# Fused block-sparse attention and squared-ReLU feed-forward: the weights in eight large loads ahead of the second batch, and the last outputs in two PSUM banks

## The chip, the cores and the metric

The kernel runs on one core of one Trainium2 chip. The metric is the device time of one execution in microseconds, the median of three runs. A profile is one further execution, recorded by the hardware profiler.

## The reference

Attention with a block mask comes first: a query block of 32 rows sees its neighbours, the first and last block, and three sampled blocks; the first and last block see all. Then a feed-forward network with a squared ReLU:

```python
# q, k, v: (4, 8, 768, 64) f32; w_in: (512, 2048); w_out: (2048, 512)
scores = scale * np.matmul(q, k.transpose(0, 1, 3, 2))
scores = np.where(mask, scores, -1000000000.0)
attn = softmax(scores)                       # written out in the reference
x = np.matmul(attn, v).transpose(0, 2, 1, 3).reshape(B * S, H * D)
h = x @ w_in
r = np.maximum(h, 0.0)
out = (r * r) @ w_out                        # (3072, 512) f32
```

## The kernel before, in words

**Attention.** A unit is one pair of heads of one batch; there are 16, numbered 0 to 15, four to a batch. Three loads of 384 KB bring a unit's q, k and v (SP's queue; `load`, L142 to L144). VectorE casts q and k to bf16 (L241), TensorE transposes them (L253), VectorE copies the transposes out of PSUM (L260) and casts v (L247; for units 1 to 3 GpSimd does that). The mask is added by 24 (or 64) more rows of the matmul's contraction; each buffer set AA, BB needs these rows once, and sets 1 to 5 get them by copies from set 0 (`static_rows`, L233 and L234). The scores of 256 queries against 256 keys, two heads (L288, L290), go through one exp on ScalarE (L295) into the product with v (L308, L310); a column of ones in VA and VB gives the softmax's sums, ScalarE forms their inverse (L317 to L319) and VectorE multiplies (L328, L329) into xT, the transposed input of the feed-forward. There are 144 such score steps, nine to a unit. In the first batch the four units alternate by query range; afterwards one unit follows another.

**Feed-forward.** xT is cut in nine token tiles T0 to T8: three of 256 tokens for batch 0, two of 384 for each later batch. For each of 16 column blocks f of w_in, `hidden` (L343) is four matmuls into one of two PSUM buffers of the pool `h`, which the transposes also use; VectorE takes max(h, 0) into one of four `r` buffers (L349); GpSimd squares it into `g` (L355). For each 128 tokens, `output` (L363) is 16 matmuls in four parts into the one PSUM buffer `y`; ScalarE copies it out (L368) and SP stores it (L372).

**Weights.** w_in and w_out are read as f32 and cast to bf16 by the DMA itself, which only GpSimd's queue issues. There are 8 loads for w_in (L273) and 8 for w_out (L276), 256 KB each as they land. A GpSimd load takes one of eight semaphores; the ninth load waits until the first has landed.

**What sets the order.** A planner in the kernel (`run_schedule`) holds one task for each of these steps with its engine, an estimated duration, what it depends on, buffers taken and given back, and a key. It always takes the task that can start first on its model clock, and among equals the lowest key; attention has lower keys than the feed-forward, so that the feed-forward fills gaps. The order is fixed when the program is built: on the chip, each engine takes its instructions strictly in that order, and waits at each for what it needs.

Of the kernel before, what the change touches and what calls it, by code (L numbers as in the profile page):

```python
# [12 lines left out]
F32 = mybir.dt.float32  # L13
BF = mybir.dt.bfloat16
# [5 lines left out]
P = 128  # L20
# [5 lines left out]
def kernel(  # L26
# [16 lines left out]
    nc = tc.nc  # L43
# [4 lines left out]
    d_model = H * D  # L48
# [4 lines left out]
    HP = H // 2  # L53
    NF = d_ff // P
# [11 lines left out]
    ps_o = ctx.enter_context(tc.psum_pool(name="ps_o", bufs=1))  # L66
    ps_h = ctx.enter_context(tc.psum_pool(name="ps_h", bufs=2))
    ps_y = ctx.enter_context(tc.psum_pool(name="ps_y", bufs=1))
    ctx.enter_context(tc.manual_schedule())


# [2 lines left out]
    tasks = []  # L74

    class Task:
        def __init__(self, eng, us, key, fn, deps=(), get=None, put=(), after=0.0, late=0.0):
            self.eng, self.us, self.key, self.fn = eng, us, key, fn
            self.deps, self.get, self.put = list(deps), get, list(put)
            self.after, self.late = after, late  # L80
            self.end = self.free = None
            self.order = len(tasks)
            self.holds = 0
            for t in self.put:
                t.holds += 1
            tasks.append(self)
# [14 lines left out]
                    r = max(r, old.free)  # L101
            return r

    def run_schedule(free, bufs):

        taken = {name: [] for name in bufs}
        left = {e: [t for t in tasks if t.eng == e] for e in free}
        while any(left.values()):
            best = None
            for e, ts in left.items():  # L110
                cand = [(max(r, free[e]), t) for t in ts
                        for r in (t.ready(taken, bufs),) if r is not None]
                if cand:
                    at = min(c[0] for c in cand)
                    t = min((c[1] for c in cand if c[0] <= at + 1e-9), key=lambda t: (t.key, t.order))
                    if best is None or at < best[0]:
                        best = (at, t)
            assert best is not None, "no task can start"
            at, t = best
            t.end = free[t.eng] = at + t.us  # L120
            if t.get:
                taken[t.get].append(t)
            for p in t.put:
                p.holds -= 1
                p.free = max(p.free or 0.0, t.end + t.late)
            left[t.eng].remove(t)
            t.fn()
        return max(free.values())
# [102 lines left out]
    def static_rows(i):  # L231

        nc.sync.dma_start(out=AA[i][64:64 + nb], in_=AA[0][64:64 + nb])  # L233
        nc.sync.dma_start(out=BB[i][0:64], in_=BB[0][0:64])  # L234
# [29 lines left out]
    w_out_sb = consts.tile([P, NF, d_model], BF, name="w_out_sb")  # L264
    wiv = moe_w_in.rearrange("(k p) f -> p k f", p=P)
    wov = moe_w_out.rearrange("(n p) d -> p n d", p=P)
    NWP = 8

    def w_load(i):

        if i < NWP:
            fs = slice(i * d_ff // NWP, (i + 1) * d_ff // NWP)
            nc.gpsimd.dma_start(out=w_in_sb[:, :, fs], in_=wiv[:, :, fs])  # L273
        else:
            n0 = (i - NWP) * 2
            nc.gpsimd.dma_start(out=w_out_sb[:, n0:n0 + 2, :], in_=wov[:, n0:n0 + 2, :])  # L276


    ptile, stile, otile, rtile, xT = {}, {}, {}, {}, {}
# [59 lines left out]
    def hidden(T, f):  # L339
        b, c0, w = T  # L340
        ph = ps_h.tile([P, TWM], F32, name="ph", tag="h")[:, 0:w]
        for kc in range(KM):
            nc.tensor.matmul(ph, w_in_sb[:, kc, f * P:(f + 1) * P], xT[b][:, kc, c0:c0 + w],  # L343
                             start=(kc == 0), stop=(kc == KM - 1))
        htile[T, f] = ph
# [6 lines left out]
    def square(T, f):  # L352
# [2 lines left out]
        G.tensor_mul(out=g, in0=r, in1=r)  # L355
        gtile[T, f] = g

    def output(T, ts, part):
        if part == 0:
            ytile[T, ts] = ps_y.tile([P, d_model], F32, name="py", tag="y")  # L360
        py = ytile[T, ts]
        for f in range(part * NF // NY, (part + 1) * NF // NY):
            nc.tensor.matmul(py, gtile[T, f][:, ts * P:(ts + 1) * P], w_out_sb[:, f, :],  # L363
                             start=(f == 0), stop=(f == NF - 1))
# [22 lines left out]
    pe = dict(late=0.2)  # L387
# [5 lines left out]
    ev, cv, sc_of, va_of, mu = {}, {}, {}, {}, {}  # L393
    for u in range(NU):
        sc_of[u], va_of[u] = [], []
    wl, tr = {}, {}

    def prepare(u):
        s0 = first[u]
        if u < HP:  # L400
            ld_t = None
        else:

            ld_t = Task("SP", 1.3, s0 - 20, (lambda u=u: load(u, nc.sync)),
                        deps=cv[u - HP] + tr[u - HP], late=6.5)
        c = {}
        tr[u] = []
        old = sc_of[u - NPB] if u >= NPB else []
        for w in (1, 0):
            kw = dict(deps=[ld_t] + old) if ld_t else dict(after=arrive[u][w])  # L410
            c[w] = Task("DVE", 0.57, s0 - 6, (lambda u=u, w=w: cast_qk(u, w)), get="qc", **kw, **SEM)
            tr[u].append(c[w])
        ev[u] = []
        for w in (1, 0):
            t = Task("PE", 0.34, s0 - 4 - w, (lambda u=u, w=w: transp(u, w)), deps=[c[w]],
                     get="h", put=[c[w]], **pe)
            for h in range(2):
                ev[u].append(Task("DVE", 0.57, s0 - 4, (lambda u=u, w=w, h=h: evac(u, w, h)),
                                  deps=[t], put=[t], **SEM))
        kw = dict(deps=[ld_t]) if ld_t else dict(after=arrive[u][2])  # L420
        kw.setdefault("deps", [])
        if u >= NPB:
            kw["deps"] += va_of[u - NPB]
        vfull = u in range(1, HP)
        cv[u] = [Task("POOL" if vfull else "DVE", 0.9 if vfull else 0.36, s0 - 2,
                      (lambda u=u, h=h: cast_v(u, h)), **kw, **SEM) for h in range(2)]
        if u == HP - 1:

            for i in range(2 * NWP):
                wl[i] = Task("POOL", 1.15, s0 + i, (lambda i=i: w_load(i)),  # L430
                             deps=cv[u], late=4.0 + 0.8 * i)
        if HP <= u < NPB:
            early = [Task("SP", 0.9, s0 - 8, (lambda u=u: static_rows(u)), after=36.0, late=5.0),
                     Task("POOL", 0.7, s0 - 8, (lambda u=u: init_v(G, u)), after=36.0, **SEM)]
        else:
            early = []
        return early
# [27 lines left out]
    for k, T in enumerate(TILES + [None]):  # L465
        hs = [(T, f) for f in range(NF)] if T else []
        ys = [(TILES[k - 1], ts, part) for ts in range(TILES[k - 1][2] // P) for part in range(NY)] if k else []
        both = [((i + 0.5) / len(hs), 0, x) for i, x in enumerate(hs)]
        both += [((i + 0.5) / len(ys), 1, x) for i, x in enumerate(ys)]
        for _, kind, x in sorted(both, key=lambda e: e[:2]):  # L470
            n_key += 1
            T_ = x[0]
            b, c0, w = T_
            if kind == 0:
                f = x[1]
                need = [mu[b * HP + a, qi] for a in range(HP)
                        for qi in range(c0 // QW, (c0 + w - 1) // QW + 1)]
                hh = Task("PE", SQ[w][0], n_key, (lambda x=x: hidden(*x)), deps=need + [wl[f // 2]],
                          get="h", **pe)
                rr = Task("DVE", SQ[w][1], 0, (lambda x=x: relu(*x)), deps=[hh], get="r", put=[hh], **SEM)  # L480
                sq_of[x] = Task("POOL", SQ[w][2], n_key, (lambda x=x: square(*x)), deps=[rr], get="g",
                                put=[rr], **SEM)
            else:
                _, ts, part = x
                fs = range(part * NF // NY, (part + 1) * NF // NY)
                last_ts = ts == w // P - 1
                yy = Task("PE", 0.862, n_key, (lambda x=x: output(*x)),
                          deps=[sq_of[T_, f] for f in fs] + [wl[NWP + f // 2] for f in fs] + ([yprev] if part else []),
                          get=None if part else "y", put=[sq_of[T_, f] for f in fs] if last_ts else [], **pe)
                yprev = yy  # L490
                if part == 0:
                    yhead = yy
                if part == NY - 1:
                    yc = Task("ACT", 0.59, 0, (lambda T_=T_, ts=ts: out_copy(T_, ts)), deps=[yy], get="ys",
                              put=[yhead], **SEM)
                    Task("SP", 0.5, 0, (lambda T_=T_, ts=ts: store(T_, ts)), deps=[yc], put=[yc], late=2.0)

    run_schedule({"PE": 6.0, "DVE": 5.1, "ACT": 7.8, "POOL": 9.0, "SP": 12.0},
                 {"ps": 2, "po": 1, "h": 2, "y": 1, "pT": PT_BUFS, "r": R_BUFS, "g": G_BUFS, "ys": 3,
                  "qc": 3})  # L500


# [28 lines left out]
```

## Time and profile before

| | |
|---|---|
| median of 3 runs | 351.83 us (351.08 to 352.35) |
| the profiled execution, its own time | 353.31 us |
| its span, first to last instruction | 351.6 us |
| TensorE (PE) busy | 318.0 us, 90% |
| ScalarE (ACT) busy | 209.9 us, 60% |
| VectorE (DVE) busy | 183.6 us, 52% |
| GpSimd (POOL) busy | 136.2 us, 39% |
| mean granted TensorE clock | 0.975 |
| DMA moved | 31.10 MB |

The profile's page gives busy shares over the whole span, a strip of 40 slices of 8.8 us, and the costliest groups of instructions with the idle time before them. The chain of waits is followed back from the last instruction to what released each. Busy time of PE counts a matmul to its modelled end: a 256-column matmul lasts 0.27 us there, though the next one can start 0.11 us later, so PE can lose time while it counts as busy. Matmuls of different kinds are therefore counted, and multiplied by their spacing, where PE's work is needed.

### The profile page before, as it was taken

Reading aid. Unit: us, or ns where it says so; the run is one execution under the profiler, and the core shown is the slowest. Engines: PE = TensorE matmul, PEld = TensorE weight load, DVE = VectorE, ACT = ScalarE, POOL = GpSimd, SP = SyncE. Lnnn points to the kernel's source line nnn. Section 1 sums busy time; section 2 is a strip of 40 time slices with the busy share of each in tenths; the row PEclk is TensorE's granted clock in tenths of the full one; section 3 lists DMA queues with packets and bytes.
Section 4 is the critical chain, followed back from the end, with each engine's and each line's share of the span. In section 5 each row is a group of like instructions: output and inputs, shape, how many; then the busy total and the mean of one; then the engine's idle time right before and its main releaser. Section 6 shows DMA issues by size and latency. Waiting matters only on the chain.

```text
span 351.6 us, 5958 instructions
## 1 busy us (share of the span) xinstructions
PE 318.0 (90%) x2306; PEld 219.3 (62%) x2306; DVE 183.6 (52%) x378; ACT 209.9 (60%) x315; POOL 136.2 (39%) x191
## 2 busy tenths in 40 slices
PE   2878850889999999999999999999999999999994
PEld 1656730666878777767777667676766755555541
DVE  7779301797867676449695433434343354444310
ACT  3688780178777686877768786787878732100011
POOL 8354125311635233105444323233233345666610
PEclk9999985699999999999999999999999999999999
DMA  7999999716622220010000000000000000010011
GB/s 249 274 323 300 285 270 206 165 59 211 208 93 79 88 76 0 34 52 8 1 2 0 32 30 2 30 32 0 33 30 3 30 32 30 30 62 30 32 60 60
DMA packets 23556, 31.10 MB, mean 88 GB/s; under 512 B 1584, under 2 KB 20016, under 8 KB 23528
## 3 DMA queue, kind: packets, MB, share of 16 engines
q1 hardware_dynamic: 16856, 26.13, 23.0%
q0 software_dynamic: 6400, 4.20, 8.0%
q8 instruction: 18, 0.29, 0.4%
q10 hardware_dynamic: 272, 0.39, 0.3%
q14 instruction: 10, 0.08, 0.1%
HBM read 27.26 MB, written 6.29 MB: 95 GB/s over the span
## 4 chain that ended last, share of the span: by engine, by line
PE 76%; DMA 11%; POOL 3%; ACT 3%; DVE 3%; SPq 2%; issue 1%; ACTq 0%; DVEq 0%
PE py L363 23%; PE ph L343 22%; DMA w_in_sb<-in_moe_w_in_dram 8%; PE po L308 8%; PE po L310 7%; PE ps L288 7%; PE ps L290 7%; DMA vs<-in_v_dram 2%; PE pt L253 2%; POOL w_in_sb L273 2%; ACT pT L295 1%; POOL g L355 1%; DVE r L349 1%; ACT ys L368 1%; SPq L233 0%
## 5 line engine op out<-in xcount | busy, mean ns | idle before, releaser
L295 ACT ACTIVATE pT<-ps 128x1024 bf16<-128x1024 f32 x144 | 141.8, 1017 | 65.1 <-PE po L310 57.1
L355 POOL TENSOR_TENSOR g<-r 128x384 bf16<-128x384 f32 (+1 forms) x144 | 111.0, 778 | 166.2 <-DVE r L349 166.1
L349 DVE TENSOR_SCALAR r<-ph 128x384 f32<-128x384 f32 (+1 forms) x144 | 73.1, 512 | 117.3 <-PE ph L343 79.6
L343 PE MATMUL ph<-xT,w_in_sb 128*128 128x384 bf16 (+1 forms) x576 | 104.0, 310 | 1.6 <-DMA w_in_sb<-in_moe_w_in_dram 1.0
L363 PE MATMUL py<-w_out_sb,g 128*128 128x512 bf16 x384 | 97.8, 381 | 1.7 <-ACT ys L368 1.4
L288 PE MATMUL ps<-AA 88*128 88x256 bf16 x288 | 73.8, 279 | 3.9 <-ACT pT L295 2.6
L343 PEld LDWEIGHTS <-w_in_sb 128*128 128x128 bf16 x576 | 56.2, 98 | 29.1 <-DMA w_in_sb<-in_moe_w_in_dram 1.2
L290 PE MATMUL ps<-BB 128*128 128x256 bf16 x288 | 73.5, 279 | 0.5 <-DVE BB L260 0.3
L308 PE MATMUL po<-pT,VA 128*128 128x256 bf16 x288 | 70.9, 274 | 3.2 <-ACT pT L295 2.3
L310 PE MATMUL po<-pT,VB 128*128 128x256 bf16 x288 | 70.9, 274 | 0.0
L363 PEld LDWEIGHTS <-g 128*128 128x128 bf16 x384 | 37.4, 98 | 34.2 <-issue 2.3
L368 ACT COPY ys<-py 128x512 f32<-128x512 f32 x24 | 14.1, 586 | 58.7 <-PE py L363 58.7
L308 PEld LDWEIGHTS <-VA 128*128 128x128 bf16 x288 | 28.2, 98 | 13.3 <-issue 4.3
L290 PEld LDWEIGHTS <-BB 128*128 128x128 bf16 x288 | 28.9, 100 | 10.4 <-issue 3.9
L288 PEld LDWEIGHTS <-AA 88*128 88x128 bf16 x288 | 28.8, 100 | 8.7 <-POOL VB L174 1.5
L310 PEld LDWEIGHTS <-VB 128*128 128x128 bf16 x288 | 28.2, 98 | 9.2 <-issue 1.6
L253 PE MATMUL pt<-identb,qc 128*128 128x128 bf16 x192 | 17.6, 236 | 13.4 <-DVE qc L241 13.3
L328 DVE TENSOR_TENSOR xT<-po,rs 64x256 bf16<-64x256 f32 x48 | 19.9, 414 | 16.9 <-ACT rs L319 16.1
L253 PEld LDWEIGHTS <-qc 128*128 128x128 bf16 x192 | 14.1, 106 | 17.6 <-DVE qc L241 16.1
L260 DVE COPY AA<-pt 64x768 bf16<-64x768 bf16 x32 | 17.6, 549 | 11.9 <-PE pt L253 11.3
L317 ACT ACTIVATE ls<-po 64x256 f32<-64x256 f32 x48 | 18.3, 381 | 7.7 <-PE po L310 6.6
L319 ACT ACTIVATE rs<-ls 128x256 f32<-128x256 f32 x48 | 20.0, 416 | 1.5
(46 smaller groups left out, 126.3 us busy)
## 6 DMA issues: line engine op xcount, KB each, us to landing
qs<-in_q_dram SPq DMA_DIRECT2D x16, 384.0 KB, 5.3
vs<-in_v_dram SPq DMA_DIRECT2D x16, 384.0 KB, 7.0
out_dram<-ys SPq DMA_DIRECT2D x24, 256.0 KB, 2.0
ks<-in_k_dram SPq DMA_DIRECT2D x15, 384.0 KB, 5.1
w_in_sb<-in_moe_w_in_dram POOLq DMA_DIRECT2D x8, 256.0 KB, 19.4
w_out_sb<-in_moe_w_out_dram POOLq DMA_DIRECT2D x8, 256.0 KB, 17.3
BB<-BB SPq DMA_DIRECT2D x5, 192.0 KB, 9.5
ks<-in_k_dram ACTq DMA_DIRECT2D x1, 384.0 KB, 3.0
```

The source lines that it names most:

```text
L253: nc.tensor.transpose(pt[:, n * P:(n + 1) * P], src[:, n, :, :].rearrange("p t d -> p (t d)"), identb)
L288: nc.tensor.matmul(ps[:, c, 0, :], KA[i][0:64 + nb, ksl], QA[i][0:64 + nb, qsl], start=True, stop=True)
L290: nc.tensor.matmul(ps[:, c, 1, :], KB[i][:, ksl], QB[i][:, qsl], start=True, stop=True)
L295: nc.scalar.activation(out=pT, in_=stile.pop((u, qi, cp)), func=AF.Exp, scale=scale)
L308: nc.tensor.matmul(po[:, 0, :], VA[i][:, n, :], pT[:, c, 0, :], start=first, stop=last, skip_group_check=True)
L310: nc.tensor.matmul(po[:, 1, :], VB[i][:, n, :], pT[:, c, 1, :], start=False, stop=last, skip_group_check=True)
L319: nc.scalar.activation(out=rs, in_=ls, func=AF.Exp, scale=-1.0)
L328: V.tensor_mul(out=xT[b][0:D, a, qsl], in0=po[0:D, 0, :], in1=rs[0:D, :])
L343: nc.tensor.matmul(ph, w_in_sb[:, kc, f * P:(f + 1) * P], xT[b][:, kc, c0:c0 + w], start=(kc == 0), stop=(kc == KM - 1))
L349: V.tensor_scalar(out=r, in0=htile.pop((T, f)), scalar1=0.0, scalar2=None, op0=AOP.max)
L355: G.tensor_mul(out=g, in0=r, in1=r)
L363: nc.tensor.matmul(py, gtile[T, f][:, ts * P:(ts + 1) * P], w_out_sb[:, f, :], start=(f == 0), stop=(f == NF - 1))
```

## The change

The weights come in eight loads instead of sixteen, of 512 KB as they land: four for w_in (512 columns each), four for w_out (four row blocks each). They are issued after GpSimd's casts of unit 2's v instead of unit 3's. A new step on SP, `loads_gate`, copies one element of the third w_out piece into a scratch tensor in DRAM; that copy waits for the third w_out load, and all loads from unit 4 on stand behind it on SP's queue. The planner gets a model of DMA transfers that follow one another (`dma`, `dma_free`) in place of fixed delays (`late`). In the last token tile, the second group of 128 tokens takes its output buffer from the pool `h` instead of `y`. Line numbers of the changed file are up to 15 higher than those of the profile.

```diff
-    def run_schedule(free, bufs):
+    def run_schedule(free, bufs, dma_free):
...
             t.end = free[t.eng] = at + t.us
+            if t.dma:
+                dma_free = max(dma_free, t.end) + t.dma
+                t.end = dma_free
...
-    NWP = 8
+    NWP = 4
...
-            n0 = (i - NWP) * 2
-            nc.gpsimd.dma_start(out=w_out_sb[:, n0:n0 + 2, :], in_=wov[:, n0:n0 + 2, :])
+            ns = slice((i - NWP) * NF // NWP, (i - NWP + 1) * NF // NWP)
+            nc.gpsimd.dma_start(out=w_out_sb[:, ns, :], in_=wov[:, ns, :])
+
+    def loads_gate():
+
+        nc.sync.dma_start(out=scratch, in_=w_out_sb[0:1, (NWP - 2) * NF // NWP, 0:1])
...
+    def y_pool(T, ts):
+
+        return "h" if T == TILES[-1] and ts % 2 else "y"
+
     def output(T, ts, part):
         if part == 0:
-            ytile[T, ts] = ps_y.tile([P, d_model], F32, name="py", tag="y")
+            pool, tag = (ps_h, "h") if y_pool(T, ts) == "h" else (ps_y, "y")
+            ytile[T, ts] = pool.tile([P, d_model], F32, name="py", tag=tag)
...
             ld_t = Task("SP", 1.3, s0 - 20, (lambda u=u: load(u, nc.sync)),
-                        deps=cv[u - HP] + tr[u - HP], late=6.5)
+                        deps=cv[u - HP] + tr[u - HP] + gate, late=2.0, dma=3.9)
...
-        if u == HP - 1:
+        if u == HP - 2:
 
             for i in range(2 * NWP):
-                wl[i] = Task("POOL", 1.15, s0 + i, (lambda i=i: w_load(i)),
-                             deps=cv[u], late=4.0 + 0.8 * i)
+                wl[i] = Task("POOL", 1.2, s0 + i, (lambda i=i: w_load(i)), deps=cv[u], late=2.0, dma=3.5)
+            gate.append(Task("SP", 0.5, 0, loads_gate, deps=[wl[2 * NWP - 2]], late=0.0))
...
-                hh = Task("PE", SQ[w][0], n_key, (lambda x=x: hidden(*x)), deps=need + [wl[f // 2]],
+                hh = Task("PE", SQ[w][0], n_key, (lambda x=x: hidden(*x)), deps=need + [wl[f * NWP // NF]],
```

GpSimd's queue before, from the casts of unit 2's v (VA_103, VB_104) to the first squares (g); VA_111 to VB_116 are the value buffers of sets 4 and 5, filled with ones:

```order
L247 CAST VA_103<-vs 128x6x64
L247 CAST VB_104<-vs 128x6x64
L247 CAST VA_107<-vs 128x6x64
L247 CAST VB_108<-vs 128x6x64
L273 DMA w_in_sb<-in_moe_w_in_dram 128x4x256 x8
L276 DMA w_out_sb<-in_moe_w_out_dram 128x2x512 x8
L173 MEMSET VA_111 128x6x64
L174 MEMSET VB_112 128x6x64
L173 MEMSET VA_115 128x6x64
L174 MEMSET VB_116 128x6x64
L355 TENSOR_TENSOR g<-r 128x256 x48
```

The same place in the changed program (line numbers shifted; VA_106 is unit 2's, VA_110 unit 3's, VA_114 to VB_119 sets 4 and 5):

```order
L253 CAST VA_106<-vs 128x6x64
L253 CAST VB_107<-vs 128x6x64
L279 DMA w_in_sb<-in_moe_w_in_dram 128x4x512 x3
L253 CAST VA_110<-vs 128x6x64
L253 CAST VB_111<-vs 128x6x64
L279 DMA w_in_sb<-in_moe_w_in_dram 128x4x512
L282 DMA w_out_sb<-in_moe_w_out_dram 128x4x512 x4
L365 TENSOR_TENSOR g<-r 128x256 x2
L179 MEMSET VA_114 128x6x64
L180 MEMSET VB_115 128x6x64
L179 MEMSET VA_118 128x6x64
L180 MEMSET VB_119 128x6x64
```

Three weight loads have moved ahead of unit 3's casts, there are eight in all, and the first two squares stand ahead of the memsets. Before, each of the eight w_out loads waits for the w_in load eight places ahead of it to land; in the changed program no weight load waits for another.

SP's queue before, from unit 3's mask rows (AA3, BB3) on; the loads of units 4 to 9 (18 loads) follow at once, and the mask rows of sets 4 and 5 stand behind them:

```order
L233 DMA AA3_105<-AA0_93 24x1536
L234 DMA BB3_106<-BB0_94 64x1536
L142 DMA qs_262<-in_q_dram 128x2x384
L143 DMA ks_263<-in_k_dram 128x2x384
L144 DMA vs_264<-in_v_dram 128x2x384
L142 DMA qs_285<-in_q_dram 128x2x384
```

and in the changed program:

```order
L239 DMA AA3_108<-AA0_96 24x1536
L240 DMA BB3_109<-BB0_97 64x1536
L239 DMA AA4_112<-AA0_96 24x1536
L240 DMA BB4_113<-BB0_97 64x1536
L239 DMA AA5_116<-AA0_96 24x1536
L240 DMA BB5_117<-BB0_97 64x1536
L286 DMA scratch_78<-w_out_sb_161 1x1
L148 DMA qs_745<-in_q_dram 128x2x384
L149 DMA ks_746<-in_k_dram 128x2x384
L150 DMA vs_747<-in_v_dram 128x2x384
```

The mask rows of sets 4 and 5 have moved ahead, and unit 4's loads stand behind the copy out of w_out.

VectorE's queue in the changed program, from the relus of T0's last and T1's first column blocks on: the casts and copies of unit 4 (L247, then L266 into AA_112 and BB_113, then L253):

```order
L359 TENSOR_SCALAR r<-ph 128x256 x3
L247 CAST qc<-ks 128x768
L247 CAST qc<-qs 128x768
L359 TENSOR_SCALAR r<-ph 128x256
L338 TENSOR_TENSOR xT_297<-po,rs 64x256
L339 TENSOR_TENSOR xT_297<-po,rs 64x256
L266 COPY AA_112<-pt 64x768
L266 COPY BB_113<-pt 64x768
L266 COPY AA_112<-pt 64x768
L266 COPY BB_113<-pt 64x768
```

Before, the same work for units 4 and 5 stands ahead of T0's first relu; in the changed program it stands behind all 16 of T0's relus, and the work for units 5 to 9 follows it.

More of the change, by code (lines that the diff above doesn't have):

```diff
@@ L68 @@
     ps_y = ctx.enter_context(tc.psum_pool(name="ps_y", bufs=1))
+    dram = ctx.enter_context(tc.tile_pool(name="dram", bufs=1, space=bass.MemoryType.DRAM))
+    scratch = dram.tile([1, 1], BF, name="scratch")
     ctx.enter_context(tc.manual_schedule())
@@ L76, with __init__ @@
     class Task:
-        def __init__(self, eng, us, key, fn, deps=(), get=None, put=(), after=0.0, late=0.0):
+        def __init__(self, eng, us, key, fn, deps=(), get=None, put=(), after=0.0, late=0.0, dma=0.0):
             self.eng, self.us, self.key, self.fn = eng, us, key, fn
@@ L80, in __init__ @@
             self.after, self.late = after, late
+            self.dma = dma
             self.end = self.free = None
@@ L395 @@
         sc_of[u], va_of[u] = [], []
-    wl, tr = {}, {}
+    wl, tr, gate = {}, {}, []
     def prepare(u):
@@ L426, in prepare @@
                       (lambda u=u, h=h: cast_v(u, h)), **kw, **SEM) for h in range(2)]
-        if u == HP - 1:
+        if u == HP - 2:
             for i in range(2 * NWP):
-                wl[i] = Task("POOL", 1.15, s0 + i, (lambda i=i: w_load(i)),
-                             deps=cv[u], late=4.0 + 0.8 * i)
+                wl[i] = Task("POOL", 1.2, s0 + i, (lambda i=i: w_load(i)), deps=cv[u], late=2.0, dma=3.5)
+            gate.append(Task("SP", 0.5, 0, loads_gate, deps=[wl[2 * NWP - 2]], late=0.0))
         if HP <= u < NPB:
-            early = [Task("SP", 0.9, s0 - 8, (lambda u=u: static_rows(u)), after=36.0, late=5.0),
+            early = [Task("SP", 0.9, s0 - 8, (lambda u=u: static_rows(u)), after=36.0, late=2.0, dma=1.0),
                      Task("POOL", 0.7, s0 - 8, (lambda u=u: init_v(G, u)), after=36.0, **SEM)]
@@ L487 @@
                 yy = Task("PE", 0.862, n_key, (lambda x=x: output(*x)),
-                          deps=[sq_of[T_, f] for f in fs] + [wl[NWP + f // 2] for f in fs] + ([yprev] if part else []),
-                          get=None if part else "y", put=[sq_of[T_, f] for f in fs] if last_ts else [], **pe)
+                          deps=[sq_of[T_, f] for f in fs] + [wl[NWP + f * NWP // NF] for f in fs] + ([yprev] if part else []),
+                          get=None if part else y_pool(T_, ts), put=[sq_of[T_, f] for f in fs] if last_ts else [], **pe)
                 yprev = yy
@@ L499 @@
                  {"ps": 2, "po": 1, "h": 2, "y": 1, "pT": PT_BUFS, "r": R_BUFS, "g": G_BUFS, "ys": 3,
-                  "qc": 3})
+                  "qc": 3}, dma_free=20.0)
 _INS = ['q', 'k', 'v', 'sampled_blocks', 'moe_w_in', 'moe_w_out']
```

## The prediction

> **What bounds the kernel now.** The page's strip of 40 slices comes first: PE's busy tenths and the clock granted to it.
>
> ```profile
> PE   2878850889999999999999999999999999999994
> PEclk9999985699999999999999999999999999999999
> ```
>
> PE is the bound: from the tenth slice (79 us) to the last but one it is full. Before that the strip shows one hole, the sixth and seventh slice (44 to 62 us), and the clock is down in the sixth to eighth. The second view is the chain of waits there (start, length, what):
>
> ```profile
> 28.59 28.63 DMA w_in_sb<-in_moe_w_in_dram
> ...
> 57.50 0.71 POOL w_out_sb L276
> ...
> 61.35 1.07 DVE qc L241
> 62.47 0.82 PE pt L253 x6
> ```
>
> and the third is the timeline of the engines that it names (start, length, engine; in brackets the idle time before and its end):
>
> ```profile
> 17.22 0.83 POOL L247 CAST VB<-vs 128x384 bf16<-128x384 f32 x1
> ...
> 23.21 6.15 POOL L273 DMA_DIRECT2D w_in_sb<-in_moe_w_in_dram  x8
> 32.90 0.70 POOL L276 DMA_DIRECT2D w_out_sb<-in_moe_w_out_dram  x1 [3.53 <-DMA w_in_sb<-in_moe_w_in_dram]
> 36.35 0.71 POOL L276 DMA_DIRECT2D w_out_sb<-in_moe_w_out_dram  x1 [2.75 <-DMA w_in_sb<-in_moe_w_in_dram]
> ```
>
> ```profile
> 60.32 0.99 DVE L349 TENSOR_SCALAR r<-ph 128x256 f32<-128x256 f32 x2 [14.15 <-POOL g L355]
> ```
>
> ```profile
> 34.57 0.60 PE L343 MATMUL ph<-xT,w_in_sb 128*128 128x256 bf16 x4
> ...
> 62.47 0.82 PE L253 MATMUL pt<-identb,qc 128*128 128x128 bf16 x6 [11.79 <-DVE qc L241]
> ```
>
> GpSimd issues eight w_in loads at 23.2 and then stands at each w_out load until a w_in load has landed, the last time until 57.5. The squares are queued behind it. With no square done, the four `r` buffers fill, VectorE stands 14.15 us in front of its next relu, the casts of unit 6 stand behind that relu, and PE waits 11.79 us for them, though ScalarE and the loaded data are there. The weights are what is late, and what they hold up is GpSimd's queue.
>
> **What the stretch loses.** PE's instructions from 34 us (its first feed-forward matmul) to 90 us:
>
> ```profile
> L290 PE MATMUL ps<-BB 128*128 128x256 bf16 x51 | 13.7, 290 | 0.0
> L288 PE MATMUL ps<-AA 88*128 88x256 bf16 x50 | 13.4, 290 | 1.0 <-ACT pT L295 1.0
> L310 PE MATMUL po<-pT,VB 128*128 128x256 bf16 x45 | 11.5, 285 | 0.0
> L308 PE MATMUL po<-pT,VA 128*128 128x256 bf16 x45 | 11.3, 282 | 1.9 <-ACT pT L295 1.6 <-DVE xT L329 0.2
> L343 PE MATMUL ph<-xT,w_in_sb 128*128 128x256 bf16 x64 | 9.9, 288 | 1.6 <-DMA w_in_sb<-in_moe_w_in_dram 1.0 <-DVE BB L260 0.5
> L253 PE MATMUL pt<-identb,qc 128*128 128x128 bf16 x48 | 4.5, 242 | 11.8 <-DVE qc L241 11.8
> L363 PE MATMUL py<-w_out_sb,g 128*128 128x512 bf16 x12 | 4.1, 464 | 0.2 <-POOL g L355 0.2
> ```
>
> Their spacing at full clock is read from the chain at 71.6 us, where they stand back to back:
>
> ```profile
> 71.58 0.34 PE pt L253 x6
> 71.91 0.86 PE py L363 x4
> 72.78 0.44 PE ph L343 x4
> ...
> 73.51 0.11 PE ps L288
> ```
>
> So 191 matmuls of attention at 0.11 are 21.0 us, 64 of `hidden` at 0.11 are 7.0, 48 transposes at 0.057 are 2.7, 12 of `output` at 0.215 are 2.6: 33.3 us of work in 56 us. 22.7 us are lost: 11.8 in the stall, the rest in half clock and short waits.
>
> **The change part by part.** *The weight loads.* GpSimd ends unit 2's casts at 17.22 + 0.83 = 18.05, 5.2 us before its present first issue. Eight issues at 6.15/8 = 0.77 us cost 6.2 us in place of 16; none waits. The squares are then free from about 29 us, before the first `hidden` at 34.6: the chain quoted above has no first link left, and the 11.8 us go. What is late next can be the weights, or the loads held behind them. Rates, from stretches of the trace (the last two columns: busy share of the DMA engines, GB/s as landed):
>
> ```profile
> 28.00:46.00 18.00, 14.13 (x124) 11.33 (x123) 10.53 (x24) 15.71 (x23) 4.18 (x6) 1.00 1.21 286
> 52.00:62.00 10.00, 0.00 (x0) 0.00 (x0) 1.50 (x3) 0.19 (x1) 5.76 (x12) 0.61 1.29 206
> ```
>
> From 28 to 46 loads of units and weights share the engines; the weights' part, from the two landings at 32.90 and 36.35, is 262 KB in 3.45 us, 76 GB/s. From 52 to 62 only weights move: 206 GB/s. When does the first byte come?
>
> ```profile
> DMA to landing us min/median/max: 9.4/19.4/28.6
> vs<-in_v_dram SPq DMA_DIRECT2D x16, 384.0 KB, 7.0
> ```
>
> The quickest w_in load landed 9.4 us after its issue, 3.45 of them its transfer, so 6 us pass first: 18 + 6 = 24. By then SP's queue holds only the mask rows, and I take 206 GB/s: a piece of 524 KB every 2.55 us. w_out's first piece lands at 24 + 5 x 2.55 = 37, the third, which opens the gate, at 42, the last at 44.5. PE's new order needs the first one after eight `hidden` (3.5 us) and eight attention steps at 0.44, at 34.6 + 7.0 = 41.6, and each next one 5 us or more later. So the weights cost nothing, with 4 us to spare.
>
> *The gate.* The one-element copy moves nothing; what is queued behind it on SP is every load from unit 4 on, and for these wait VectorE's casts and the transposes. Unit 4's three loads issue at 42 to 43.5 and land by 50, taking the 7.0 us of the row above. PE's order has, between its first `hidden` and unit 4's first transpose, 27 attention steps (11.9 us), 18 `hidden` (7.9) and three quarters of an output (2.6): 22.4 us, to 57 at the earliest. 7 us to spare; with 7.0 us for each following unit (57, 64, 71) the transposes of units 5 to 7 (from 64, 68 and 72 by the same counting) just have their data. Cost nothing; without that cover, every us of delay is a us of PE.
>
> *What stays lost.* Two things in the same stretch. Up to unit 4's transpose ScalarE is nearly the bound: 15 exps and five inverses of the first batch. Its own row, and VectorE's:
>
> ```profile
> L295 ACT ACTIVATE pT<-ps 128x1024 bf16<-128x1024 f32 x144 | 141.8, 1017 | 65.1 <-PE po L310 57.1
> L241 DVE CAST qc<-qs 128x768 bf16<-128x768 f32 x16 | 12.1, 755 | 0.1
> L241 DVE CAST qc<-ks 128x768 bf16<-128x768 f32 x16 | 10.9, 681 | 1.9 <-DMA ks<-in_k_dram 1.5
> L260 DVE COPY BB<-pt 64x768 bf16<-64x768 bf16 x32 | 17.8, 560 | 0.6
> L247 DVE CAST VB<-vs 128x384 bf16<-128x384 f32 x13 | 7.7, 595 | 0.0
> L349 DVE TENSOR_SCALAR r<-ph 128x256 f32<-128x256 f32 x48 | 19.9, 422 | 30.5 <-PE ph L343 15.6 <-POOL g L355 14.2
> L329 DVE TENSOR_TENSOR xT<-po,rs 64x256 bf16<-64x256 f32 x48 | 20.5, 427 | 0.6
> ```
>
> 15 x 0.985 (141.8/144) and five inverses at about 1.2 are 20.8 us against PE's 22.4; two engines so close, each in fixed order, lose some to each other. Bounds: 1 us, and 5, which would be PE busy for only 80% of that stretch; I take 3. Second, the work of units 4 to 9 on VectorE, which the old order spread over 25 to 85 us, now comes in one run. From unit 4's first cast to unit 9's: five units of 1.44 (casts) + 2.24 (four copies) + 0.9 (two casts of v, 0.6 at most each), one cast, ten relus at 0.42, six normalizations of two at 0.43: 22.9 + 0.7 + 4.2 + 5.2 = 33 us. PE has 33 attention steps (14.5), ten transposes (3.4), nine `hidden` (4.0) and seven quarters (6.0) there, 27.9. PE waits for the difference, 5 us; if the casts took only the copies' 0.56, 3; with hand-offs 8. New losses 3 + 5 = 8, in place of 22.7: 14.7 us gained.
>
> *Half clock.* The clock before and at the hole:
>
> ```profile
> 42.00:47.30 5.30, 3.38 (x30) 2.63 (x28) 0.84 (x2) 5.04 (x8) 0.71 (x1) 1.00 1.21 286
> 47.30:50.50 3.20, 3.20 (x17) 2.10 (x14) 0.00 (x0) 2.48 (x4) 0.70 (x1) 0.50 1.23 295
> ```
>
> It fell at 47.3, before the stall, after a stretch in which PE worked 3.3 us of 5.3 by the spacing. The sum above has no half clock after 34 us; PE's load there is 80% and more. A stretch like 42 to 47.3 elsewhere would cost up to 1.7 us per 3.4 us. The Trainium skill (TensorE: Matmul & The Clock Gate, "Part 1: The HAM clock gate") has half rate come after an idle window of some 3.4 us. The trace disagrees: no wait before 47.3 was that long. By the skill's rule the sum stands; by the row one such window may come on top.
>
> *The tail.* The last three outputs now:
>
> ```profile
> 335.37 3.61 PE L363 MATMUL py<-w_out_sb,g 128*128 128x512 bf16 x16
> ...
> 339.70 3.61 PE L363 MATMUL py<-w_out_sb,g 128*128 128x512 bf16 x16 [0.72 <-ACT ys L368]
> ...
> 344.03 3.61 PE L363 MATMUL py<-w_out_sb,g 128*128 128x512 bf16 x16 [0.72 <-ACT ys L368]
> ```
>
> With the second group in a bank of pool `h` and its parts interleaved with the first's, the second waits for no copy, and the third's copy (0.6 us) runs beside the last quarter of the second (0.86). 1.4 us gained; bounds 0 and 1.4.
>
> *The sum.* 14.7 + 1.4 = 16.1 us off the profiled execution's 353.31: 337.2. That execution was 1.5 us above the median, so 351.83 - 16.1 = 335.7. Since PE is full from 79 us on before, and has the same work left after, what is gained by then is kept to the end. With the low bounds (4 lost) 331.7, with the high (13 lost, no tail) 342.1.
>
> **The rivals.** *VectorE becomes the bound* (the bunched casts, or ScalarE in front of them, cost more than the upper bounds): for it speaks VectorE's 33 us against 28, against it that the squares no longer stop it. At twice my 8 us, 16 lost, the time is 343.7.
>
> *Half clock comes back* in the thinner part of the first batch, as the row at 42 to 47.3 allows: two windows of 3.4 us cost up to 3.4 us, 339.1. Against it: PE then has the feed-forward to fill its gaps, which it lacked at 42.
>
> *The other side: the gate becomes the stall.* If the software queue doesn't run faster alone (its 76 GB/s is its own pace, not its share), seven pieces of 524 KB take 48 us, the gate opens at 72, unit 4 lands at 79, and PE waits from 60 to 80: 335.7 + 20 = 356. It decides from a landing of unit 4 past 76. The 206 GB/s of the row at 52 to 62 speaks plainly against it; for it only that this row is the only one with the queue alone.
>
> *It doesn't do what it says:* the eight loads still hold GpSimd, for instance behind unit 3's v. Then the squares are late as before and the time stays within 1 us. The order shows no wait between weight loads.
>
> **How the numbers follow.** Forecast 0.72, VectorE 0.11, half clock 0.09 (inside the forecast's range), the gate 0.05, nothing 0.03. The range 330 to 344 takes in the bounds and the first two rivals, and leaves out about 0.13: the last two and the far end of VectorE's case. About 0.3% is what a measurement of this kernel can tell from no change: faster 0.91, same 0.03, slower 0.06.
>
> **What would show it.** GpSimd's eight issues end before 30 us with no wait between them; the first square follows the first relu within 1 us; no PE wait above 3 us after 34 us; the granted clock stays 1.0 from 34 us on; unit 4's casts wait for no DMA; VectorE near 100% busy between 60 and 90 us; no wait of PE for the output copy in the last 15 us. A PE wait for unit 4's or 5's cast that ends with a DMA would make the prediction wrong, and so would a first output that waits for w_out.

## The result, and the profile after

| | before | changed |
|---|---|---|
| median | 351.84 us (351.08 to 352.35, 4 runs) | 334.23 us (333.92 to 334.62, 4 runs) |
| ratio | | 0.9502, 95% interval 0.9481 to 0.9522 |
| profiled execution, its span | 353.31, 351.6 us | 334.62, 332.9 us |
| mean granted TensorE clock | 0.975 | 0.998 |

The change takes 17.6 us off, 5.0%; the prediction was 335.7 us, 16.1 us off. The strip of the changed kernel's page (40 slices, now of 8.3 us):

```profile
PE   2876999999899999899999999999999999999994
PEclk9999999999999999999999999999999999999999
```

The hole is gone and so is the dip of the clock. PE is full from the fifth slice (33 us), where the feed-forward starts, and no longer from the tenth. GpSimd's and SP's timelines show how (start, length; in brackets the idle time before and what ended it):

```profile
18.77 2.43 POOL L279 DMA_DIRECT2D w_in_sb<-in_moe_w_in_dram  x3
...
24.23 0.74 POOL L279 DMA_DIRECT2D w_in_sb<-in_moe_w_in_dram  x1
24.96 2.98 POOL L282 DMA_DIRECT2D w_out_sb<-in_moe_w_out_dram  x4
36.74 1.19 POOL L365 TENSOR_TENSOR g<-r 128x256 bf16<-128x256 f32 x2 [8.80 <-DVE r L359]
```

```profile
43.56 0.26 SPq L286 DMA_DIRECT2D scratch<-w_out_sb  x1
43.92 0.38 SPq L148 DMA_DIRECT2D qs<-in_q_dram  x1
```

GpSimd has issued its eight loads by 27.9 us, none waiting for another; it then waits 8.8 us for the first relu, in place of the relus waiting for it. The gate opens at 43.56 and unit 4's loads follow. The same groups of PE's matmuls from 34 to 90 us as the prediction shows of before:

```profile
L298 PE MATMUL ps<-AA 88*128 88x256 bf16 x68 | 16.9, 273 | 1.3 <-ACT pT L305 1.3
L300 PE MATMUL ps<-BB 128*128 128x256 bf16 x68 | 16.9, 273 | 0.0
L318 PE MATMUL po<-pT,VA 128*128 128x256 bf16 x63 | 15.4, 272 | 0.3 <-ACT pT L305 0.3
L320 PE MATMUL po<-pT,VB 128*128 128x256 bf16 x62 | 15.1, 272 | 0.0
L353 PE MATMUL ph<-xT,w_in_sb 128*128 128x256 bf16 x108 | 14.9, 272 | 0.0
L378 PE MATMUL py<-w_out_sb,g 128*128 128x512 bf16 x34 | 9.3, 379 | 0.3
L259 PE MATMUL pt<-identb,qc 128*128 128x128 bf16 x72 | 5.8, 219 | 0.5 <-DVE r L359 0.5
```

In this profile 31 of the 2306 matmul records are missing, but none of the weight loads (PEld), one of which goes with each matmul. They show 40 matmuls of `output` where the table has 34:

```profile
L378 PEld LDWEIGHTS <-g 128*128 128x128 bf16 x40 | 3.9, 97 | 2.6
```

With the spacings of the prediction and the counts of the weight loads this is 260 x 0.11 + 108 x 0.11 + 40 x 0.215 + 72 x 0.057 = 53.2 us of work in 56, against 33.3 before: 19.9 us more. Of 22.7 lost us, 2.8 are left. Three smaller things go beside it. By 34 us PE has done 0.7 us less than before (the transposes of units 4 and 5 are not among its work yet), the tail gives 0.7 us, and two waits behind 90 us that were not there before take 1.3, the longer one for a product on VectorE:

```profile
138.23 0.27 PE L318 MATMUL po<-pT,VA 128*128 128x256 bf16 x1 [1.15 <-DVE xT L339]
```

19.9 - 0.7 + 0.7 - 1.3 = 18.6 us, and the spans differ by 18.7.

### The profile page after: what moved, and what is told of

Read it like the earlier page. It is cut to its first block, busy times and chain, and to the rows that moved or that the text cites. A ratio compares the mean times of both kernels' runs of the same rounds, so it can differ in the third digit from the quotient of the medians.

```text
span 332.9 us, 5925 instructions
## 1 busy us (share of the span) xinstructions
PE 310.9 (93%) x2275; PEld 217.4 (65%) x2306; DVE 179.7 (54%) x378; ACT 209.6 (63%) x315; POOL 128.9 (39%) x183
## 4 chain that ended last, share of the span: by engine, by line
PE 71%; DVE 10%; ACT 7%; DMA 7%; issue 4%; POOL 1%; DVEq 0%; ACTq 0%; SPq 0%
PE py L378 22%; PE ph L353 21%; PE po L318 7%; PE po L320 7%; PE ps L298 6%; PE ps L300 6%; ACT pT L305 4%; DMA qs<-in_q_dram 3%; DMA ks<-in_k_dram 2%; DVE qc L247 2%; DVE r L359 2%; DMA AA<-AA 2%; DVE AA L266 2%; DVE BB L266 1%; PE pt L259 1%
## 5 line engine op out<-in xcount | busy, mean ns | idle before, releaser
L378 PE MATMUL py<-w_out_sb,g 128*128 128x512 bf16 x353 | 91.5, 379 | 2.3 <-ACT ys L383 0.7
L298 PE MATMUL ps<-AA 88*128 88x256 bf16 x288 | 72.7, 276 | 4.6 <-ACT pT L305 3.4
L300 PE MATMUL ps<-BB 128*128 128x256 bf16 x288 | 72.4, 276 | 0.5 <-DVE BB L266 0.3
L338 DVE TENSOR_TENSOR xT<-po,rs 64x256 bf16<-64x256 f32 x48 | 19.8, 413 | 17.4 <-ACT rs L329 16.1
L327 ACT ACTIVATE ls<-po 64x256 f32<-64x256 f32 x48 | 18.2, 380 | 7.9 <-PE po L320 6.8
L339 DVE TENSOR_TENSOR xT<-po,rs 64x256 bf16<-64x256 f32 x48 | 20.5, 428 | 0.6
L266 DVE COPY AA<-pt 64x768 bf16<-64x768 bf16 x32 | 17.5, 548 | 6.2 <-PE pt L259 5.3
L328 ACT ACTIVATE ls<-po 64x256 f32<-64x256 f32 x48 | 18.0, 375 | 0.6
```

The lines of the kernel that those rows point to most:

```text
L266: V.tensor_copy(out=dst[h * D:(h + 1) * D, :], in_=pt[h * D:(h + 1) * D, :])
L298: nc.tensor.matmul(ps[:, c, 0, :], KA[i][0:64 + nb, ksl], QA[i][0:64 + nb, qsl], start=True, stop=True)
L300: nc.tensor.matmul(ps[:, c, 1, :], KB[i][:, ksl], QB[i][:, qsl], start=True, stop=True)
L339: V.tensor_mul(out=xT[b][D:P, a, qsl], in0=po[D:P, 1, :], in1=rs[D:P, :])
```

## The experiments

All ratios are to the kernel before, run beside it on the same chip.

**Which half of the change does it: the eight loads, or the order of the loads?** Two kernels, each with one half.

*Eight loads alone*, in the old place and with nothing else moved: `w_load` issues at every second step, a piece of double size.

```diff
+        if i % 2:
+            return
         if i < NWP:
-            fs = slice(i * d_ff // NWP, (i + 1) * d_ff // NWP)
+            fs = slice(i * d_ff // NWP, (i + 2) * d_ff // NWP)
...
-            nc.gpsimd.dma_start(out=w_out_sb[:, n0:n0 + 2, :], in_=wov[:, n0:n0 + 2, :])
+            nc.gpsimd.dma_start(out=w_out_sb[:, n0:n0 + 4, :], in_=wov[:, n0:n0 + 4, :])
```

> The kernel before with its weights in eight loads of 512 KB at the same place of GpSimd's queue; nothing else moves, loads of units 4 to 9 share the DMA engines as before. Theory (GpSimd standing in front of the w_out loads is what stalls the kernel; which loads go first matters less): GpSimd is free at 30 us, the 11.8 us wait of TensorE for a cast is gone, a wait of up to 4 us for a weight piece may come in its place; 339 to 344 us. Rival (the weights' landing is the stall, whoever waits for it, so they must go first): TensorE waits 6 us or more for w_in or w_out instead, 345 to 350 us.

Measured: 340.23 us (ratio 0.969, 0.9659 to 0.9722). GpSimd's loads, and the longest wait left on PE after 30 us:

```profile
22.09 3.16 POOL L275 DMA_DIRECT2D w_in_sb<-in_moe_w_in_dram  x4
25.21 3.00 POOL L278 DMA_DIRECT2D w_out_sb<-in_moe_w_out_dram  x4
```

```profile
52.30 1.02 PE L365 MATMUL py<-w_out_sb,g 128*128 128x512 bf16 x3 [3.27 <-DMA w_out_sb<-in_moe_w_out_dram]
```

GpSimd is free at 28 us and the wait for a cast is gone; 3.3 us of it come back at the first output, whose weights still share the engines with the loads of units 4 to 9. This half alone is worth 11.3 us.

*Sixteen loads, but early and behind the gate*: the changed kernel with each load cut in two, and so with GpSimd's waits back.

```diff
+            for j in range(2 * i, 2 * i + 2):
+                fs = slice(j * d_ff // (2 * NWP), (j + 1) * d_ff // (2 * NWP))
+                nc.gpsimd.dma_start(out=w_in_sb[:, :, fs], in_=wiv[:, :, fs])
...
+            for j in range(2 * (i - NWP), 2 * (i - NWP) + 2):
+                ns = slice(j * 2, (j + 1) * 2)
+                nc.gpsimd.dma_start(out=w_out_sb[:, ns, :], in_=wov[:, ns, :])
```

> The changed kernel with each 512 KB load cut in two again: sixteen loads of 256 KB, the ninth to sixteenth waiting for the first to eighth to land, the gate kept, every other instruction in the same order. Theory (with the engines to themselves the weights move at 206 GB/s, so the last wait on GpSimd ends by about 38 us, when the first squares come): within 1 us of the changed kernel, 334 to 335.5 us. Rival (the number of loads is what matters): GpSimd is late again, 340 us or more.

Measured: 334.82 us (ratio 0.9536, 0.9496 to 0.9577), the changed kernel's time within its spread. The first and the last w_out load on GpSimd:

```profile
26.09 0.70 POOL L284 DMA_DIRECT2D w_out_sb<-in_moe_w_out_dram  x1 [1.28 <-DMA w_in_sb<-in_moe_w_in_dram]
...
35.24 0.71 POOL L284 DMA_DIRECT2D w_out_sb<-in_moe_w_out_dram  x1 [0.64 <-DMA w_in_sb<-in_moe_w_in_dram]
```

GpSimd still waits at each w_out load, but some 0.6 us in place of 3, and is free at 36 us, when the first relu comes. So the number of loads is not what matters once the weights have the engines to themselves. Without that it is worth 11 us.

**Was GpSimd's queue the only stall before?** The kernel before, with the first eight squares of T0 on VectorE, so that nothing up to the stall depends on GpSimd:

```diff
-        G.tensor_mul(out=g, in0=r, in1=r)
+        (V if T == TILES[0] and f < 8 else G).tensor_mul(out=g, in0=r, in1=r)
```

> The kernel before with the first eight squares of tile T0 on VectorE, so that neither relus nor casts depend on GpSimd during its weight loads; weight loads as before. If GpSimd's queue alone is the stall, TensorE's 11.8 us wait at 50.5 us goes and the time falls to about 341 us. If the weights' landing is a second limit right behind it, TensorE stops at its first output instead, until w_out's first piece lands at 58.5 us (32.9 + 25.6): 4 us gained at most, 347 to 350 us.

Measured: 348.99 us (ratio 0.9928, 0.9904 to 0.9953). PE's timeline in the place of the old stall:

```profile
58.41 0.59 PE L363 MATMUL py<-w_out_sb,g 128*128 128x512 bf16 x1 [7.49 <-DMA w_out_sb<-in_moe_w_out_dram]
```

The wait for the casts is gone and 7.5 us of waiting for w_out itself stand in its place. There were two stalls, one behind the other, and late weights behind both; an edit that frees only the squares uncovers the second.

**What is the gate worth?** The changed kernel without the one-element copy; everything else in the same order.

```diff
     def loads_gate():
-        nc.sync.dma_start(out=scratch, in_=w_out_sb[0:1, (NWP - 2) * NF // NWP, 0:1])
+        pass
```

> The changed kernel without the one-element copy, so that the loads of units 4 to 7 start at about 20 us instead of 44 and share with the weights; every other instruction in the same order. Theory (the gate buys the weights' landing): w_out's first piece lands near 46 us instead of near 40, TensorE, which needs it at 43, waits some 3 us, and the next pieces are on time: 336 to 339 us. Rival (the gate buys nothing): 334 us, the same as the changed kernel.

Measured: 341.54 us (ratio 0.9725, 0.9696 to 0.9753), 7 us above the changed kernel and 2.5 above what the theory allowed. PE's wait, and the stretches during and behind it (the last three columns: granted clock, DMA share, GB/s):

```profile
47.41 0.58 PE L378 MATMUL py<-w_out_sb,g 128*128 128x512 bf16 x1 [4.33 <-DMA w_out_sb<-in_moe_w_out_dram]
```

```profile
43.10:45.70 2.60, 0.00 (x0) 0.00 (x0) 0.89 (x3) 1.07 (x2) 1.21 (x3) 1.00 1.16 265
45.70:47.40 1.70, 0.00 (x0) 0.00 (x0) 0.00 (x0) 0.00 (x0) 0.00 (x0) 0.50 1.14 266
47.40:51.00 3.60, 3.36 (x13) 1.87 (x14) 0.00 (x0) 0.00 (x0) 0.00 (x0) 0.50 1.16 271
50.00:56.00 6.00, 6.00 (x43) 4.64 (x42) 1.80 (x5) 4.25 (x7) 1.19 (x2) 0.79 1.17 256
```

The wait is where the theory put it, 4.3 us in place of 3. The rest is the clock: it is half from within the wait until 52.5 us (0.79 over six us is 2.5 us at half), so that 5.1 us of PE's work behind the wait go at half speed, another 2.5 us. 4.3 + 2.5 explain 6.8 of the 7.3 us. PE's instructions stand in the same order in both kernels, and one by one they confirm it: without the gate they come 4.3 us later at the end of the wait, 6.8 us later from 52.5 us on, and 6.8 us later at the end. The gate pays, and a wait of 4 us costs more than 4 us. The Trainium skill (TensorE: Matmul & The Clock Gate, "Part 1: The HAM clock gate") has half rate come after an idle window of about 3.4 us. The trace agrees in part: the wait is longer than that, but the clock fell 2.6 us into it, at 45.7 us.

Without the gate the changed kernel (341.54 us) is also no faster than eight loads alone in the old place (340.23, measured beside it). Early issue gains nothing here without the gate, at least in an order that was planned with it.

**How early must the weights be?** All eight loads behind unit 3's casts; the planner orders the rest anew.

```diff
-        if u == HP - 2:
+        if u == HP - 1:
```

> The changed kernel with all eight weight loads behind unit 3's casts instead of unit 2's; the planner orders the rest by it. Theory (there are about 4 us to spare between w_out's first landing and its first use, and the weights come some 4 to 5 us later): a wait of at most 1.5 us for w_out, 334 to 336 us. Rival (the early issue is what keeps TensorE fed): 338 us or more.

Measured: 336.04 us (ratio 0.9553, 0.9524 to 0.9583). The theory's size holds, its mechanism is not seen. The first w_out load is issued at 26.2 us in place of 25.0 and lands at about 39.1 in place of 38.5 (by the shortest time to landing, 12.9 and 13.5 us), not 4 to 5 us later; the planner has moved the first output to 47.6 us, and PE never waits for w_out. The issue before unit 3's casts is worth under 2 us in this order; what weights that are 4 us late would cost, this run does not show.

**What is still lost.** The changed kernel was run again as a yardstick, beside three kernels with one edit each or both. In the changed kernel PE still waits 0.72 us before the third output of the last tile: the group that ScalarE copies last, at 324.46, holds the bank that it needs.

```profile
323.60 0.58 ACT L383 COPY ys<-py 128x512 f32<-128x512 f32 x1 [6.11 <-PE py L378]
324.46 0.58 ACT L383 COPY ys<-py 128x512 f32<-128x512 f32 x1 [0.28 <-PE py L378]
```

```profile
325.10 3.61 PE L378 MATMUL py<-w_out_sb,g 128*128 128x512 bf16 x16 [0.72 <-ACT ys L383]
```

The planner runs the second group first, since `h` is free earlier than `y`. First edit, the pools swapped:

```diff
-        return "h" if T == TILES[-1] and ts % 2 else "y"
+        return "h" if T == TILES[-1] and ts % 2 == 0 else "y"
```

Second edit, the casts of v of units 4 to 9 on GpSimd:

```diff
-        (G if 0 < u < HP else V).tensor_copy(out=dst, in_=vs[:, h])
+        (G if 0 < u < 10 else V).tensor_copy(out=dst, in_=vs[:, h])
```

> The changed kernel once more, as the yardstick for the three beside it: 334.2 us within 0.5.

> The changed kernel with the two PSUM pools of the last tile swapped: first and third group of 128 tokens in pool h, second in y; every instruction in the same order. In the changed kernel the third output still waits 0.72 us, because the group that is copied last holds the bank that it needs. Theory: that wait goes, 0.7 us faster, 333.5 us. Rival (the wait is the copy itself, whatever the bank): the same, 334.2 us.

> The changed kernel with the casts of v of units 4 to 9 on GpSimd instead of VectorE, at the same place of the program; TensorE, ScalarE and SP in the same order. Theory (VectorE's bunched work is what TensorE still loses 3 us to between 59 and 90 us): some 5 us less on VectorE there, 1 to 2.5 us faster, 331.7 to 333.2 us. Rival (ScalarE or the fixed order sets that loss, or the two engines' casts slow each other down): 334 us or more.

> The last two edits together. If they act at different places, as the theory has it, they add up: 331 to 332.5 us.

| kernel | median (range), us | ratio to before, interval |
|---|---|---|
| changed, again | 335.24 (334.00 to 335.49) | 0.9523, 0.9498 to 0.9549 |
| pools swapped | 333.27 (333.11 to 333.69) | 0.9476, 0.9454 to 0.9497 |
| casts on GpSimd | 333.54 (332.89 to 333.92) | 0.9480, 0.9456 to 0.9503 |
| both | 332.22 (331.76 to 332.45) | 0.9442, 0.9421 to 0.9464 |

The yardstick came out 1 us above the first runs, outside what was expected. Two stretches of its profile (the columns as above) show one reason: the first row is the stretch ahead, the second is at half clock nearly throughout. The third row is the second's stretch in the first profile of the same kernel.

```profile
24.00:26.80 2.80, 1.56 (x12) 1.16 (x11) 0.84 (x2) 2.74 (x5) 2.57 (x4) 0.92 1.22 220
26.80:30.20 3.40, 3.40 (x20) 2.48 (x19) 0.00 (x0) 2.31 (x3) 0.00 (x0) 0.56 1.24 205
```

```profile
26.80:30.20 3.40, 3.13 (x28) 2.68 (x28) 0.20 (x1) 3.40 (x5) 1.14 (x2) 1.00 1.24 206
```

In the same 3.4 us PE starts 20 matmuls and not 28. Matmul by matmul, the yardstick is 0.9 us ahead of the first profile when the clock falls and 0.6 behind from there to the end (spans 333.5 and 332.9), so the half clock costs 1.5 us. Whether it comes differs from execution to execution: three of the yardstick's five have a mean clock of 0.995, as this one, and all four of the swap have 1.000. It is not the whole reason, since one yardstick run took 335.37 us with a mean clock of 0.998, which leaves no room for such a window.

So the medians, by which the swap gives 2.0 us, the casts 1.7 and both 3.0, hold more than the edits. PE's order is the same in these kernels, and the profiles tell the edits' part. The swap's is ahead of the first profile of the changed kernel by 0.6 us from 27 us up to the tail, and by 1.5 at the last output: the swap itself gives 0.9, against 0.7 expected. In its profile the 47 recorded matmuls of the three outputs stand in one run without a wait:

```profile
316.68 10.52 PE L378 MATMUL py<-w_out_sb,g 128*128 128x512 bf16 x47
```

The casts came out at 333.54 us, 0.3 above the upper end of their theory. Their profile has the half clock of the yardstick's, from 26.3 us, and the two run alike up to 81 us. The last output's first matmul, in the yardstick and with the casts, is 1.0 us apart:

```profile
325.71 3.61 PE L378 MATMUL py<-w_out_sb,g 128*128 128x512 bf16 x16 [0.72 <-ACT ys L383]
```

```profile
324.71 3.61 PE L378 MATMUL py<-w_out_sb,g 128*128 128x512 bf16 x16 [0.72 <-ACT ys L383]
```

So the casts give 1.0 us, the least that the theory allowed: 0.3 of it by 90 us, where it put them, and the rest near 95 and 160 us. From 59 to 90 us, the changed kernel, then the casts on GpSimd (busy time of PE, PEld, DVE, ACT, POOL):

```profile
59.00:90.00 31.00, 28.95 (x263) 23.15 (x266) 29.65 (x66) 23.35 (x36) 6.79 (x10) 1.00 0.66 211
```

```profile
59.00:90.00 31.00, 29.20 (x266) 23.39 (x269) 26.92 (x54) 23.56 (x36) 13.47 (x23) 1.00 0.66 209
...
88.26 0.27 PE L298 MATMUL ps<-AA 88*128 88x256 bf16 x1 [1.16 <-ACT pT L305]
```

VectorE has 2.7 us less, PE hardly more work. A wait of 1.16 us for an exp stands there with the casts and without. That left the fixed order, so the last kernel has both edits and lets the planner know of the second:

```diff
-        vfull = u in range(1, HP)
+        vfull = u in range(1, 10)
```

> As the two edits together, but the planner knows of the casts on GpSimd and orders everything else by it. Theory (what is left of the loss between 59 and 90 us after those two edits is the fixed order: TensorE waits 1.2 us for an exp there in both profiles): 330.5 to 332 us. Rival (the order is no better for it): 332.2 us or more.

Measured: 331.19 us (331.10 to 331.23; ratio 0.9417, 0.9383 to 0.9451), the lowest median of all, though the interval overlaps that of the two edits together. The same stretch, first with the two edits, then with the planner told:

```profile
59.00:90.00 31.00, 29.20 (x266) 23.41 (x268) 26.91 (x55) 23.59 (x36) 13.05 (x22) 1.00 0.66 209
```

```profile
59.00:90.00 31.00, 30.57 (x283) 24.28 (x282) 29.81 (x61) 24.09 (x36) 12.65 (x21) 1.00 0.75 247
```

VectorE is as full as in the changed kernel (29.8 of 31 us), and PE starts 283 matmuls and not 266; its longest wait there is 0.3 us and no longer 1.16. So a full VectorE does not by itself hold PE up. That points to what stands in front of what; which of the planner's moves counts, the runs do not show.

## Why the prediction was right

- **The stall and its chain.** As predicted: GpSimd free by 28 us, squares behind the relus, no wait of PE above 1.2 us after 34 us. The runs add what the prediction had only as "the weights are what is late": two stalls stood behind each other, and either eight loads or the early place behind the gate would have freed GpSimd in time.
- **Weights and gate at no cost.** The gate opened at 43.6 (predicted 42: the first load was issued 0.7 us later than the sum had it, and landed 9.5 us behind its issue and not 8.5), and nothing waited for w_out. The rate of 206 GB/s with the engines to themselves held: 206 GB/s again in the stretch from 26.8 us. Unit 4's cast follows a relu at once, so that the loads behind the gate were not waited for:

```profile
57.38 0.42 DVE L359 TENSOR_SCALAR r<-ph 128x256 f32<-128x256 f32 x1 [1.79 <-PE ph L353]
57.83 0.56 DVE L247 CAST qc<-ks 128x768 bf16<-128x768 f32 x1
```

- **What stays lost: the right places, but put nearly three times too large.** Predicted 3 + 5 us, measured 2.8 in all by the count of weight loads: 0.4 from 34 to 59 us and 2.3 from 59 to 90. The first term set two engines of near equal load against each other and took 3 from bounds of 1 and 5; PE lost less than the lower bound. The second took VectorE's whole surplus of 5 us as PE's loss; it was 2.3, under the lower bound of 3, and at least part of that was not VectorE's load, since the planned casts do better with VectorE as full.
- **Two terms put at nothing.** That "what is gained by then is kept to the end" does not quite hold: the two new waits at 138 and 159 us take 1.3 us again. And PE starts into the stretch with 0.7 us less done.
- **The tail: wrong by half.** The second output indeed waits for no copy. That "the third's copy (0.6 us) runs beside the last quarter of the second" is the step that failed: the bank that the third output needs is that of the group copied last. One wait of 0.72 us went, not two; swapping the pools takes the other away.
- **Half clock.** The rival put it in the thin part of the first batch, and there it came, in the profiles of the yardstick and of the casts, for one window of 3.4 us, at a price of 1.5 us where the prediction had up to 1.7. In neither of the two profiles of the changed kernel did it come between 34 us and the last output.
- **The rival on the other side** fell: the software queue does run faster alone.

The mechanism was right; that 335.7 came within 1.5 us is in part luck. For the profiled execution the sum gave 337.2 and the result was 334.62, and its errors pull against each other: 5.2 us too much kept as lost on one side, 0.7 too much gained at the tail, 0.7 not foreseen ahead of 34 us and 1.3 behind 90 us on the other. Without these three the forecast would have been 5 us too slow. The medians come closer than the profiled executions because the one before stood 1.5 us above its median and the changed one only 0.4.

## What to carry to other kernels

Look at what is queued behind a DMA issue that can wait: on an engine that also computes, a wait for a free semaphore stops all that work, and the stall shows up engines away, here as PE waiting for a VectorE cast. Give transfers that everything needs the DMA engines to themselves before those that are needed later; here that mattered more than their size or number. Before an edit frees one wait, ask which transfer lands next in the same place: if it is late too, the wait only changes its name.

## What the runs showed of the hardware that was not expected

- The casting loads took 76 GB/s of the 286 while they shared, and 206 alone; the loads of units kept the larger part. Early issue on one queue is therefore not priority; the gate on the other queue is.
- A wait of PE of 4.3 us cost 6.8, since the clock was half for 5.1 us behind it. A wait of 3.27 us (eight loads alone) was followed by no half clock: 1.00 is granted from 52.3 to 55.7 us. The clock also fell without any such wait: in the yardstick's profile the longest wait in that part before it fell, at 26.4 us, was 1.24 us, and in the profile before it fell at 47.3, with waits of 0.30 and 1.62 us ahead (the prediction's "no wait before 47.3 was that long" leaves out PE's 5.27 us in front of its very first matmul). What the threshold is, these runs do not show.
- Half clock lasted 3.4 us (yardstick, 26.4 to 29.8) or 6.8 (no gate, 45.7 to 52.5); in the kernel before it was 3.4 from 47.3 and 13.7 from 54.1. In the traces' record of the clock these are 1, 2 and 4 times 3.41 us. What a fall costs depends on the work that PE has in these windows, and not on the wait alone.
